# Block attention and a gated Fourier mixer in one kernel: two heads' outputs transposed into one half-word bank, block sums regrouped, zero products given banks of their own

## The chip, the core and the metric

The kernel runs on one NeuronCore of a Trainium2 chip. That core has a matrix engine (TensorE, PE in the profile), a vector engine (VectorE, DVE), a scalar engine (ScalarE, ACT), a general engine (GpSimd, POOL), and a queue engine (SyncE, SP) that only starts transfers. Each engine executes its own instructions strictly in the order in which the program lists them; engines wait for each other through semaphores. Products of TensorE land in PSUM, which is cut into banks; everything else lives in SBUF. The metric is the device time of one execution in microseconds (us); lower is better.

## The reference: what is computed

The input is `q`, `k`, `v` of shape (4, 8, 768, 64): 4 batches of 8 heads, 768 positions, 64 values each. Per head, the keys are cut into 12 blocks of 64 positions:

```python
k_rep = k.reshape(B, H, n_blocks, block, D).mean(axis=3)      # block sums of the keys
gate_scores = np.einsum('bhsd,bhnd->bhsn', q, k_rep)          # which blocks a query likes
top_idx = np.argsort(np.where(causal, gate_scores, -1e9), axis=-1)[..., -3:]
mask = own block or one of the top 3, and key position <= query position
attn = softmax(where(mask, q @ k.T / 8, -1e9)) @ v
x = attn.transpose(0, 2, 1, 3).reshape(4, 768, 512)
proj = x @ w_proj                                             # three parts: x1, x2, x3
y = x1 * irfft(rfft(x2) * rfft(filter)) * x3                  # along the 768 positions
out = y @ w_out
```

So there are 32 heads of attention, and after every 8 heads one batch of the mixer.

## The kernel before, in words

**Heads and slots.** The order of the work is written out by hand. The kernel runs through slots; slot 3n + s is step s (0, 1 or 2) of head n, written (n, s) here. In each slot the program lists, in this order: the scores of the slot's third of head n (`scores`, four, three or two products into a two-bank PSUM tile `sps`, then one exponential `ex` on ScalarE); at s = 1 the division of the head before by its row sums (`normalise`, VectorE, which writes `xn`); at s = 2 of every even n the transposition of two finished heads (`turn_outputs`); GpSimd's zeroing of the triangle above the diagonal in `ex` (`diagonals`, line 475); the work that prepares later heads (`prepare`); the mixer's pieces (`units`); and last the product of the previous slot's `ex` with the values (`product`, into the PSUM tile `o`, line 490).

**Mixer pieces.** A table (`head_plan`) gives each of the 24 slots of eight heads its pieces of the batch that is finished: X2 (the second projection), F1 and F2 (the Fourier products there and back), X13 (first and third projection) and O (the last product). The table starts at slot (9, 0), so that heads 9 to 16, 17 to 24 and 25 to 32 have the same pieces in the same places, except that the first of these rounds has no O.

**PSUM.** Two double banks (`ps_big`) hold the scores, and at the start the sine phases `dftp`. All other results share four single banks (`ps_one`, function `one_tile`): block sums, transposes, gates, masks, `o`, and the mixer's pairs of results. A new tile takes a bank whose last readers are listed earlier, and its first product waits for those readers. Two parts of one tile are not told apart when waits are placed.

**Outputs of two heads.** `turn_outputs` (lines 509 to 518) transposes `xn` (768 positions by 2 x 64 values) with TensorE in two halves of 384 positions, each into an fp32 bank of its own. The first half is multiplied by the identity, the second by a matrix `flip16` with ones on the other diagonal, which also turns the order of positions round, as the Fourier pieces want it. ScalarE copies each half into `xT`. GpSimd makes `flip16` in slot (1, 1).

**Block sums of the keys.** For heads 0 to 11 TensorE adds the keys up: `key_sums_mm`, then `key_sums_copy` (two copies on VectorE), `key_sums_turn` (transpose) and `key_sums_split`. For heads 12 to 31 they come from a second reading of the keys: `add_blocks` has GpSimd's transfer queue add four (or two) slices of the keys of a group of heads into `k_blk` (96 rows of 16 x 64 values), one transfer at the end of one of the heads listed in `by_block`; `fold_blocks` and `sum_blocks` halve the 16 slices down to one on VectorE (lines 325, 331, 335); `turn_blocks` transposes the result into `krt` (line 340, TensorE); `split_blocks` writes the two fp16 parts that `gate` multiplies with the queries. Groups: heads 12 to 15 (2 transfers), 16 to 23 (4), 24 to 31 (4). For a group that starts at head f the fold stands at (f - 3, 0), the sum at (f - 3, 1), the transpose at (f - 3, 2) and the split at (f - 2, 0): heads 9, 13 and 21.

**Gate and mask.** `gate` (at (n, 1), n even, for heads n + 2 and n + 3) picks the blocks on VectorE; `turn_mask` transposes the result into the bank `gmp`, and two copies (line 440) put it into the tile `qkT` of each of the two heads. Up to head 11 it stands at (n, 0), n odd, both copies on ScalarE; later at (n, 1), the second copy on VectorE.

**Zero products.** `warm` (line 755) multiplies zeros at the start, 5, 2 and 2 times. It writes the unused half of the second `dftp` tile. VectorE's `phase_round` (line 209) and `sines` (line 223) read and write the `dftp` tiles.

Of the kernel before, what the change touches and what calls it, by code (L numbers as in the profile page):

```python
# [12 lines left out]
ALU = mybir.AluOpType  # L13
# [4 lines left out]
def kernel(  # L18
# [30 lines left out]
    fp = FP16  # L49

    const = ctx.enter_context(tc.tile_pool(name="const", bufs=1))
# [21 lines left out]
    def one_tile(name, shape=(P, 512)):  # L73
        return ps_one.tile(list(shape), FP32, name=name, tag="one", padded_shape=[P, 512])
# [194 lines left out]
    def key_sums_mm(g, cs):  # L269

        w = len(key_groups[g])
        if g not in sums:
            sums[g] = one_tile("krp", (P, KG * D))
        for c in cs:
            nc.tensor.matmul(sums[g][0:NBLK, 0:w * D], lhsT=eblk[:, c, :], rhs=keys[g][:, 0:w, c, :],  # L275
                             start=(c == 0), stop=(c == SC - 1))

    def key_sums_copy(g):
        w = len(key_groups[g])
        krp = sums[g]  # L280
        krs = small.tile([NBLK, KG, 2, D], FP32, name="krs", tag="krs", bufs=1)
        nc.vector.tensor_copy(krs[:, 0:w, 0, :],
                              krp[0:NBLK, 0:w * D].rearrange("n (h d) -> n h d", h=w))
        nc.vector.tensor_copy(krs[:, 0:w, 1, :], krs[:, 0:w, 0, :])
        sums[g] = krs

    def key_sums_turn(g):
# [23 lines left out]
    HB = H * NBLK  # L311

    def add_blocks(j, i):
        first, w, parts, _ = by_block[j]
        b, h = divmod(first, H)
        src = k[b, h:h + w].rearrange("h (x t) d -> (h x) t d", t=64 // parts)
        if i == 0:
            blocks[j] = kpool.tile([HB, KP, D], FP32, name="k_blk", tag="k_blk", bufs=2)
        nc.gpsimd.dma_start(out=blocks[j], in_=src[:, i * KP:(i + 1) * KP, :],
                            accum_op=ALU.add if i else ALU.bypass)  # L320

    def fold_blocks(j):
        kb = blocks[j]
        m = KP // 2
        nc.vector.tensor_add(kb[:, 0:m, :], kb[:, 0:m, :], kb[:, m:KP, :])

    def sum_blocks(j):
        kb = blocks[j]
        m = KP // 4
        while m > 1:  # L330
            nc.vector.tensor_add(kb[:, 0:m, :], kb[:, 0:m, :], kb[:, m:2 * m, :])
            m //= 2
        krs = small.tile([HB, 2, D], FP32, name="krb", tag="krb", bufs=1)
        for i in range(2):
            nc.vector.tensor_add(krs[:, i, :], kb[:, 0, :], kb[:, 1, :])
        blocks[j] = krs
# [4 lines left out]
        blocks[j] = krt  # L341

    def split_blocks(j):
        first, w, parts, _ = by_block[j]
# [164 lines left out]
    def turn_outputs(m, xT):  # L509

        xn = xns.pop(m)
        for half in range(2):
            xp = one_tile("xp", (P, HALF))
            for i in range(HC):
                at_ = i if half == 0 else HC - 1 - i
                nc.tensor.matmul(xp[:, P * at_:P * (at_ + 1)], lhsT=xn[:, HC * half + i, :],
                                 rhs=flip16 if half else id_f16, start=True, stop=True)
            nc.scalar.copy(xT[:, m % DC, HALF * half:HALF * (half + 1)], xp)

# [229 lines left out]

    def warm(times):

        for _ in range(times):
            nc.tensor.matmul(phases["big", 1][:, 512:1024], lhsT=gm16s[1][:, 1, :],
                             rhs=gm16s[1][:, 2:SC, :].rearrange("p c s -> p (c s)"),
                             start=True, stop=True, skip_group_check=True)

    flip16 = const.tile([P, P], fp)
# [61 lines left out]

    def prepare(n, s):

        if s == 0:
            for m in key_loads.get(n, [n + 6]):
                if m < NH:
                    load_key(m)
            for m in [11, 12] if n == 6 else [n + 5] if n < 6 else [n + 6]:
                if m < NH:
                    load_query(m)  # L830
            if n + 2 < NH:
                load_value(n + 2)
        if n < 2:
            prepare_first(n, s)
        elif s == 0:
            if n % 2 == 1 and n + 1 < PE_HEADS:
                turn_mask([n + 1, n + 2], [nc.scalar.copy] * 2)
            if n + 2 in group_at:
                key_sums_turn(group_at[n + 2])
                key_sums_split(group_at[n + 2])  # L840
            if n == 2:
                turn_both(5)
            for j, group in enumerate(by_block):
                if n + 2 == group[0]:
                    split_blocks(j)
            if n + 4 < PE_HEADS:
                ready_query(n + 4)
            for j, group in enumerate(by_block):
                if n + 3 == group[0]:
                    fold_blocks(j)  # L850
        elif s == 1:
            if n in (6, 8, 10):
                spectrum(n // 2 - 3)
            if PE_HEADS <= n + 4 < NH:
                turn_query(n + 4)
            if PE_HEADS <= n + 5 < NH:
                cast_key(n + 5)
            if n % 2 == 0 and n < NH - 2:
                gate([n + 2, n + 3])
            elif PE_HEADS <= n + 1 < NH - 1:  # L860
                turn_mask([n + 1, n + 2], [nc.scalar.copy, nc.vector.tensor_copy])
            for j, group in enumerate(by_block):
                if n + 3 == group[0]:
                    sum_blocks(j)
        else:
            if n + 4 < PE_HEADS:
                turn_both(n + 4)
            if n + 1 < NH:
                cast_value(n + 1)
            for j, group in enumerate(by_block):  # L870
                for i, m in enumerate(group[3]):
                    if m == n:
                        add_blocks(j, i)

        if n > 0 and n + 3 in group_at:
            key_sums_mm(group_at[n + 3], (2 * s, 2 * s + 1))
            if s == 2:
                key_sums_copy(group_at[n + 3])

    def prepare_first(n, s):  # L880
        if (n, s) == (0, 0):
            turn_pe(1, 0, nc.vector.tensor_copy)
            gate([1])
            key_mask(2)
            ready_query(2)
            key_sums_mm(2, range(SC))
        elif (n, s) == (0, 1):
            turn_mask([1], [nc.scalar.copy])
            ready_query(3)
            key_sums_copy(2)  # L890
            key_sums_turn(2)
            turn_both(2)
            key_sums_split(2)
            for i in range(1, NB):
                nc.gpsimd.memset(v16s[i][:, :, D:DV], 1.0)
        elif (n, s) == (0, 2):
            turn_both(3)
            ready_query(4)
            cast_value(1)
        elif (n, s) == (1, 0):  # L900
            gate([2, 3])
        elif (n, s) == (1, 1):
            turn_both(4)
            ready_query(5)
            nc.gpsimd.memset(flip16, 0.0)
            nc.gpsimd.affine_select(
                out=flip16, in_=flip16, compare_op=ALU.not_equal,
                fill=1.0, base=-(P - 1), pattern=[[1, P]], channel_multiplier=1)
        else:
            turn_mask([2, 3], [nc.scalar.copy] * 2)  # L910
            cast_value(2)
# [3 lines left out]
    for slot in range(max(units) + 1):  # L915
# [32 lines left out]
        if s == 2:  # L948
            if PE_HEADS <= n + 5 < NH:
                cast_query(n + 5, nc.scalar.copy)  # L950
            for j, group in enumerate(by_block):
                if n + 3 == group[0]:
                    turn_blocks(j)

        pn, ps = divmod(slot - 1, 3)
# [36 lines left out]
```

## Time and profile before

| | |
|---|---|
| median of 3 runs | 269.45 us (268.19 to 270.83) |
| profiled execution: its own time | 268.72 us |
| profiled execution: span of the instructions | 267.0 us, mean granted TensorE clock 0.98 |
| busy: TensorE | 237.2 us (89% of the span) |
| busy: VectorE / ScalarE / GpSimd | 197.8 / 182.1 / 170.4 us |
| data moved | 41.05 MB, 154 GB/s on average |
| ScalarE's copies of the transposed outputs (line 518) | 32 of 485 ns |

The span runs from the first to the last instruction of the program; the execution's own time has 1.7 us around it. "Busy" adds up the time in which an engine had an instruction in work. In the lists of instructions, a row gives the start, the duration, engine and line, what is written and read, a count, and in brackets how long the engine stood idle before and who ended that wait. "PEld" is TensorE's loading of weights, which runs beside its products.

### The profile page before, as it was taken

The page shows a single profiled execution, that of the slowest core. Times are in us where ns is not written, and L with a number is a line of the kernel's source. Part 1 is how long each engine was busy: PE and PEld are TensorE (multiplying, and loading weights), DVE is VectorE, ACT ScalarE, POOL GpSimd, SP SyncE. Part 2 cuts the span into 40 slices and gives each one's busy share as a digit, 9 for nine tenths or more (in the row PEclk, how much of TensorE's full clock was granted, in tenths as well). Part 3 has the DMA queues.
Part 4 walks back from the last instruction along what each step waited for, and adds up shares of the span by engine and source line. Part 5 has one row for each costly group of instructions (what it writes and reads, how often), then busy time and mean ns, then how long its engine had stood idle before and what let it go on. Part 6 is the DMA issues. An engine that isn't in the chain of part 4 may idle for free.

```text
span 267.0 us, 6284 instructions
## 1 busy us (share of the span) xinstructions
PE 237.2 (89%) x2214; PEld 144.5 (54%) x2214; DVE 197.8 (74%) x592; ACT 182.1 (68%) x283; POOL 170.4 (64%) x326
## 2 busy tenths in 40 slices
PE   7778888989788888699999988999999999999994
PEld 3447655646445555466565554565555655554641
DVE  4875798887779889976787999677878635588730
ACT  3545786879878676768887766887866785522463
POOL 5635666677735788779866986877567657228330
PEclk9897999999999999979999999999999999999999
DMA  8977876999799999988999995898382120110056
GB/s 166 217 118 206 209 169 114 185 164 200 122 227 163 180 187 199 221 181 179 195 191 239 201 203 128 204 222 193 73 195 74 26 79 2 39 39 2 0 198 237
DMA packets 115232, 41.05 MB, mean 154 GB/s; under 512 B 107328, under 2 KB 110400, under 8 KB 115200
## 3 DMA queue, kind: packets, MB, share of 16 engines
q1 hardware_dynamic: 110880, 34.61, 62.0%
q0 software_dynamic: 4320, 6.03, 14.2%
q8 instruction: 17, 0.28, 0.5%
q14 instruction: 15, 0.12, 0.2%
HBM read 28.57 MB, written 6.29 MB: 131 GB/s over the span
## 4 chain that ended last, share of the span: by engine, by line
PE 45%; DVE 22%; ACT 15%; POOL 7%; issue 7%; DMA 3%; SPq 0%; ACTq 0%; POOLq 0%; DVEq 0%
ACT ex L467 7%; PE sps L464 6%; PE op L620 6%; PE o L490 4%; PE x13b L585 4%; POOL ex L475 3%; DMA q_nat<-in_q_dram 3%; PE x2a L546 3%; PE x2b L546 3%; ACT qkT L440 3%; DVE t L570 3%; DVE t L567 2%; PE f2b L601 2%; PE krp L275 2%; DVE m L423 2%
## 5 line engine op out<-in xcount | busy, mean ns | idle before, releaser
L467 ACT ACTIVATE ex<-sps 128x1024 f16<-128x1024 f32 (+2 forms) x96 | 87.3, 918 | 44.1 <-PE sps L464 38.7
L475 POOL TENSOR_SCALAR_AFFINE_SELECT ex<-ex 128x128 f16<-128x128 f16 (+1 forms) x128 | 47.8, 387 | 58.1 <-ACT ex L467 57.2
L464 PE MATMUL sps<-qkT 76*128 76x384 f16 (+2 forms) x288 | 53.0, 292 | 0.5 <-ACT qkT L440 0.5
L490 PEld LDWEIGHTS <-ex 128*128 128x128 f16 x672 | 32.4, 99 | 20.6 <-issue 6.0
L490 PE MATMUL o<-v,ex 128*128 128x65 f16 x672 | 36.9, 195 | 3.6 <-POOL ex L475 0.9
L585 PEld LDWEIGHTS <-wp 128*128 128x128 f16 x256 | 24.5, 97 | 18.1 <-issue 4.4
L585 PE MATMUL x13b<-xT,wp 128*128 128x384 f16 x108 | 21.9, 325 | 2.2 <-DVE t L570 1.7
L464 PEld LDWEIGHTS <-qkT 76*128 76x128 f16 x288 | 20.6, 98 | 5.2 <-issue 0.8
L620 PE MATMUL op<-wo,yT 128*128 128x512 f16 x96 | 23.0, 378 | 0.0
L613 POOL TENSOR_TENSOR yT<-gx,yy 128x384 f16<-128x384 f32 x16 | 17.5, 1091 | 8.1 <-DVE yy L607 8.1
L585 PE MATMUL x13a<-xT,wp 128*128 128x384 f16 x108 | 22.0, 325 | 0.0
L574 POOL TENSOR_TENSOR PQ<-t,t 128x512 f16<-128x512 f32 x12 | 15.3, 1271 | 8.1 <-DVE t L567 7.5
L379 POOL TENSOR_SCALAR qk<-rem 128x320 f16<-128x320 f32 x32 | 15.4, 481 | 6.9 <-DVE rem L375 4.7
L590 DVE TENSOR_TENSOR gx<-x1sb,x13b 128x384 f32<-128x384 f16 x27 | 14.9, 551 | 5.8 <-ACT x1sb L589 4.8
L506 DVE TENSOR_TENSOR xn<-o,rz 128x384 f16<-128x384 f32 x32 | 17.8, 558 | 1.1
L375 DVE TENSOR_TENSOR rem<-q_nat,qk 128x320 f32<-128x320 f32 x32 | 17.3, 541 | 1.3 <-ACT qk L368 0.3
L623 ACT COPY osb<-op 128x512 f32<-128x512 f32 x24 | 14.0, 585 | 5.7 <-PE op L620 5.0
L357 POOL CAST qk<-k_nat 128x384 f16<-128x384 f32 x31 | 16.5, 534 | 0.0
L401 POOL CAST v<-v_nat 128x384 f16<-128x384 f32 x32 | 16.2, 506 | 0.1
L440 ACT COPY qkT<-gmp 12x640 f16<-12x640 f16 x22 | 15.0, 681 | 1.4 <-PE gmp L438 0.9
L575 POOL TENSOR_TENSOR PQ<-t,t 128x512 f16<-128x512 f32 x12 | 15.2, 1268 | 0.0
L546 PEld LDWEIGHTS <-xT 128*128 128x128 f16 x96 | 9.2, 97 | 9.6
(152 smaller groups left out, 483.4 us busy)
## 6 DMA issues: line engine op xcount, KB each, us to landing
q_nat<-in_q_dram SPq DMA_DIRECT2D x32, 192.0 KB, 3.9
k_nat<-in_k_dram SPq DMA_DIRECT2D x32, 192.0 KB, 4.0
v_nat<-in_v_dram SPq DMA_DIRECT2D x32, 192.0 KB, 4.0
out_dram<-osb SPq DMA_DIRECT2D x24, 256.0 KB, 2.1
k_blk<-in_k_dram POOLq DMA_DIRECT2D x10, 384.0 KB, 6.0
rows<-in_moe_filter_fft_dram SPq DMA_DIRECT2D x2, 768.0 KB, 6.6
wp<-in_moe_w_proj_dram POOLq DMA_DIRECT2D x6, 256.0 KB, 5.4
wo<-in_moe_w_out_dram POOLq DMA_DIRECT2D x2, 256.0 KB, 8.0
```

Source lines behind the costliest of these rows:

```text
L357: copy(qk16s[n % NB][:, 1, :, 0:D], keys[g][:, i])
L375: nc.vector.tensor_sub(rems[n], q_nat[:, 1:SC], qk16[:, 0, 1:SC, 0:D])
L440: copies[h](turned[n][D:D + NBLK, 0, 1:SC], gmp[64 * h:64 * h + NBLK, P:S].rearrange("n (c s) -> n c s", c=SC - 1))
L464: nc.tensor.matmul(sps[:, col:col + qe - qs], lhsT=turned[n][0:76, 1, kc, :], rhs=qT[0:76, qs:qe], start=True, stop=True, skip_group_check ...
L467: nc.scalar.activation(ex[:, lo:hi], sps[:, lo:hi], AF.Exp, bias=0.0, scale=scale)
L475: nc.gpsimd.affine_select(out=sub, in_=sub, compare_op=ALU.is_ge, fill=0.0, base=0, pattern=[[0, cnt], [1, P]], channel_multiplier=-1)
L490: nc.tensor.matmul(outs[n][:, qc * DE:(qc + 1) * DE], lhsT=ex[:, col + P * j:col + P * (j + 1)], rhs=vals[n][:, kc, 0:DE], start=(gi == 0 ...
L506: nc.vector.tensor_tensor(out=xns[n // 2][:, :, D * (n % 2):D * (n % 2 + 1)], in0=o[:, :, 0:D], in1=rz.to_broadcast([P, SC, D]), op=ALU.mult)
L546: nc.tensor.matmul(pp, lhsT=xT[:, dc, base + P * i:base + P * (i + 1)], rhs=wp[:, dc, Dm:2 * Dm], start=(dc == 0), stop=(dc == DC - 1))
L585: nc.tensor.matmul(dst, lhsT=wp[:, dc2, base:base + P], rhs=xT[:, dc2, hs:hs + HALF], start=(dc2 == 0), stop=(dc2 == DC - 1))
L613: nc.gpsimd.tensor_mul(yT[:, dc, S - 1:HALF - 1:-1], st["g"][:, dc, 1, :], yy[:, 1, :])
L620: nc.tensor.matmul(op, lhsT=yT[:, cc, P * scn:P * (scn + 1)], rhs=wo[:, cc, :], start=(cc == 0), stop=(cc == DC - 1))
```

## The change

Six edits:

1. `turn_outputs` transposes all six pieces by the identity into one fp16 tile of 768 columns, which is one bank. ScalarE copies the first 384 columns forwards and the last 384 backwards. `flip16` and the two GpSimd instructions that make it go.
2. The groups of block sums become heads 12 to 19, 20 to 27 (4 transfers each) and 28 to 31 (2). Each group names its four places: fold, sum, transpose, split. They are (9, 0), (9, 1), (9, 2), (10, 0); then (15, 0), (15, 1), (15, 2), (17, 0); then (23, 0), (23, 1), (23, 2), (25, 0). Transfers are issued at the end of heads 4, 5, 6, 7; 10, 11, 12, 13; 17, 19.
3. In a slot, fold, sum and split now stand ahead of the rest of `prepare`, so the sum is listed before the mask copies.
4. The mask of heads 10 and 11 moves from (9, 0) to (9, 1), its second copy from ScalarE to VectorE.
5. The two copies of the block sums of heads 2 and 3 move from VectorE in (0, 1) to ScalarE in (0, 0).
6. `warm` takes a single bank (`unread`) for each of its three calls.

```diff
-    by_block = [(12, 4, 2, [6, 7]), (16, 8, 1, [8, 9, 10, 11]), (24, 8, 1, [13, 15, 17, 19])]
+    by_block = [
+        (12, 8, 1, [4, 5, 6, 7], [(9, 0), (9, 1), (9, 2), (10, 0)]),
+        (20, 8, 1, [10, 11, 12, 13], [(15, 0), (15, 1), (15, 2), (17, 0)]),
+        (28, 4, 2, [17, 19], [(23, 0), (23, 1), (23, 2), (25, 0)]),
+    ]
...
-    def key_sums_copy(g):
+    def key_sums_copy(g, copy=nc.vector.tensor_copy):
...
-        for half in range(2):
-            xp = one_tile("xp", (P, HALF))
-            for i in range(HC):
-                at_ = i if half == 0 else HC - 1 - i
-                nc.tensor.matmul(xp[:, P * at_:P * (at_ + 1)], lhsT=xn[:, HC * half + i, :],
-                                 rhs=flip16 if half else id_f16, start=True, stop=True)
-            nc.scalar.copy(xT[:, m % DC, HALF * half:HALF * (half + 1)], xp)
+        xp = ps_one.tile([P, S], fp, name="xp", tag="one", padded_shape=[P, 2 * 512])
+        for c in range(SC):
+            nc.tensor.transpose(xp[:, P * c:P * (c + 1)], xn[:, c, :], id_f16)
+        nc.scalar.copy(xT[:, m % DC, 0:HALF], xp[:, 0:HALF])
+        nc.scalar.copy(xT[:, m % DC, HALF:S], xp[:, S - 1:HALF - 1:-1])
...
+        unread = one_tile("unread")
         for _ in range(times):
-            nc.tensor.matmul(phases["big", 1][:, 512:1024], lhsT=gm16s[1][:, 1, :],
+            nc.tensor.matmul(unread, lhsT=gm16s[1][:, 1, :],
...
     def prepare(n, s):
 
+        for j, group in enumerate(by_block):
+            for fn, place in zip((fold_blocks, sum_blocks, None, split_blocks), group[4]):
+                if (n, s) == place and fn:
+                    fn(j)
...
-            if n % 2 == 1 and n + 1 < PE_HEADS:
+            if n % 2 == 1 and n + 1 < 10:
                 turn_mask([n + 1, n + 2], [nc.scalar.copy] * 2)
...
-            elif PE_HEADS <= n + 1 < NH - 1:
+            elif 10 <= n + 1 < NH - 1:
                 turn_mask([n + 1, n + 2], [nc.scalar.copy, nc.vector.tensor_copy])
...
             key_sums_mm(2, range(SC))
+            key_sums_copy(2, nc.scalar.copy)
         elif (n, s) == (0, 1):
             turn_mask([1], [nc.scalar.copy])
             ready_query(3)
-            key_sums_copy(2)
...
-            nc.gpsimd.memset(flip16, 0.0)
-            nc.gpsimd.affine_select(
-                out=flip16, in_=flip16, compare_op=ALU.not_equal,
-                fill=1.0, base=-(P - 1), pattern=[[1, P]], channel_multiplier=1)
...
             for j, group in enumerate(by_block):
-                if n + 3 == group[0]:
+                if (n, s) == group[4][2]:
                     turn_blocks(j)
```

More of the change, by code (lines that the diff above doesn't have):

```diff
@@ L281, in key_sums_copy @@
         krs = small.tile([NBLK, KG, 2, D], FP32, name="krs", tag="krs", bufs=1)
-        nc.vector.tensor_copy(krs[:, 0:w, 0, :],
-                              krp[0:NBLK, 0:w * D].rearrange("n (h d) -> n h d", h=w))
-        nc.vector.tensor_copy(krs[:, 0:w, 1, :], krs[:, 0:w, 0, :])
+        copy(krs[:, 0:w, 0, :], krp[0:NBLK, 0:w * D].rearrange("n (h d) -> n h d", h=w))
+        copy(krs[:, 0:w, 1, :], krs[:, 0:w, 0, :])
         sums[g] = krs
@@ L313, in add_blocks @@
     def add_blocks(j, i):
-        first, w, parts, _ = by_block[j]
-        b, h = divmod(first, H)
-        src = k[b, h:h + w].rearrange("h (x t) d -> (h x) t d", t=64 // parts)
+        first, w, parts = by_block[j][0:3]
+        t = 64 // parts
+        src = k.rearrange("b h (x t) d -> (b h x) t d", t=t)[first * S // t:(first + w) * S // t]
         if i == 0:
@@ L343, in split_blocks @@
     def split_blocks(j):
-        first, w, parts, _ = by_block[j]
+        first, w, parts = by_block[j][0:3]
         krt = blocks.pop(j)
@@ L859, in prepare @@
                 gate([n + 2, n + 3])
-            elif PE_HEADS <= n + 1 < NH - 1:
+            elif 10 <= n + 1 < NH - 1:
                 turn_mask([n + 1, n + 2], [nc.scalar.copy, nc.vector.tensor_copy])
-            for j, group in enumerate(by_block):
-                if n + 3 == group[0]:
-                    sum_blocks(j)
         else:
@@ L870, in prepare @@
             for j, group in enumerate(by_block):
-                for i, m in enumerate(group[3]):
-                    if m == n:
-                        add_blocks(j, i)
+                if n in group[3]:
+                    add_blocks(j, group[3].index(n))
         if n > 0 and n + 3 in group_at:
@@ L951 @@
             for j, group in enumerate(by_block):
-                if n + 3 == group[0]:
+                if (n, s) == group[4][2]:
                     turn_blocks(j)
```

6 lines of the change are left out of this document (removed).

## The prediction, made before the changed kernel was run

> **What bounds the kernel now.** I read the page first, for the engines' shares:
>
> ```profile
> PE 237.2 (89%) x2214; PEld 144.5 (54%) x2214; DVE 197.8 (74%) x592; ACT 182.1 (68%) x283; POOL 170.4 (64%) x326
> ```
>
> TensorE has work in 89% of the span, and no other engine is near that. So what can go is TensorE's idle time, about 30 us, and the second view is that of its waits (total us, times, longest):
>
> ```profile
> PE krt L291 <- DVE krs L284: 3.0, 3, 1.9
> PE krt L340 <- DVE krb L335: 2.1, 2, 1.0
> ...
> PE f2b L601 <- ACT xT L518: 1.5, 3, 0.5
> PE f1b L562 <- ACT xT L518: 1.4, 4, 0.3
> ...
> PE gps L414 <- DVE krb L307: 0.9, 1, 0.9
> ```
>
> Each of these waits has an edit beside it in the diff. TensorE executes in order, so a wait in it delays all that is listed behind, the next scores first. Third came the list of instructions around each wait, fourth the granted clock in single stretches.
>
> **The change part by part**, against the profiled execution's own 268.72 us.
>
> *Zero products (edit 6).* In the list of the start:
>
> ```profile
> 3.01 2.31 PE L755 MATMUL dftp<-gm 128*128 128x512 f16 x5
> ...
> 5.36 1.02 DVE L209 TENSOR_SCALAR dft_ka<-dftp 128x384 f32<-128x384 f32 x2 [1.69 <-PE dftp L755]
> ...
> 6.64 0.86 PE L395 MATMUL tp<-id_f,qk 128*76 128x128 f16 x6
> ...
> 8.37 0.23 PE L291 MATMUL krt<-id_f,krs 12*128 12x12 f32 x1 [0.86 <-DVE krs L284]
> ```
>
> VectorE stood 1.69 us for products that nobody reads, because they share a tile with a phase. In the changed program the second and third rounding carry no wait for TensorE. VectorE's queue behind them (query, remainder, block sums) moves forward by up to 1.6 us. Next late is TensorE itself: its zero products and the transposes still end at 7.50. So `krt` comes at 7.50 instead of 8.37: **-0.85 us**. Bounds: nothing (if a later wait of the start decides) and -1.6 (the whole rounding). The three new bank users add no wait: their banks come from block sums and transposes whose readers the next TensorE instruction needs anyway.
>
> *Copies on ScalarE (edit 5).* Head 0:
>
> ```profile
> 18.43 0.92 ACT L467 ACTIVATE ex<-sps 128x896 f16<-128x896 f32 x1 [2.15 <-PE sps L464]
> ...
> 19.38 0.68 ACT L440 COPY qkT<-gmp 12x640 f16<-12x640 f16 x1
> ...
> 20.69 0.26 PE L291 MATMUL krt<-id_f,krs 12*128 12x12 f32 x2 [1.92 <-DVE krs L284]
> ...
> 22.05 0.65 PE L490 MATMUL o<-v,ex 128*128 128x65 f16 x8
> ```
>
> The sums' products are listed ahead of the scores for which the exponential at 18.43 waited, so they are done by then; but VectorE copies them only after a gate and two queries. ScalarE idles just there (2.15 us before 18.43), and the copies go there. They have 128 columns; ScalarE's copies of 384 take 485 ns (row below), so I take 0.3 us each, which push the exponential from 18.43 to about 18.6. Behind them wait the mask copy (to 20.3) and with it, by its bank, the product `o`, which thus starts at 20.3 instead of 22.05: **-1.7 us**. Bounds: -1.9 (the whole wait) and -0.5 (if VectorE's transposed copies, now first in its queue, come late for head 1).
>
> *Mask of heads 10 and 11 (edit 4).*
>
> ```profile
> 74.21 0.47 PE L438 MATMUL gmp<-id_f,gm 128*76 128x128 f16 x5 [1.02 <-DVE gm L427]
> ```
>
> At (9, 1) the gate is long done, and X2 starts without it: **-1.0 us**, bounds -0.5 and -1.4. VectorE gets one 0.49 us copy more in head 9, beside TensorE's X2.
>
> *Block sums leave heads 13 and 21 (edits 2, 3).* Starts of heads by their first exponential, with what stands between:
>
> ```profile
> 103.28 1.02 ACT L467 ACTIVATE ex<-sps 128x1024 f16<-128x1024 f32 x1 [0.90 <-POOL ex L475]
> ...
> 107.72 1.26 POOL L575 TENSOR_TENSOR PQ<-t,t 128x512 f16<-128x512 f32 x1
> ...
> 108.17 1.41 DVE L331 TENSOR_TENSOR k_blk<-k_blk 96x256 f32<-96x256 f32 x2
> ...
> 110.41 0.27 PE L340 MATMUL krt<-id_f,krb 96*128 96x96 f32 x1 [1.04 <-DVE krb L335]
> ...
> 111.44 1.83 ACT L467 ACTIVATE ex<-sps 128x1024 f16<-128x1024 f32 x2 [1.62 <-PE sps L464]
> ...
> 207.82 1.02 ACT L467 ACTIVATE ex<-sps 128x1024 f16<-128x1024 f32 x1 [1.22 <-PE sps L464]
> ...
> 214.00 1.02 ACT L467 ACTIVATE ex<-sps 128x1024 f16<-128x1024 f32 x1 [0.72 <-PE sps L464]
> ```
>
> Head 13 lasts 8.16 us (103.28 to 111.44). Head 29 has the same mixer pieces and no sums, and lasts 6.18. In heads 13 and 21 the sums stand on VectorE behind the mask copy, which waits for ScalarE, and `krt` holds TensorE for 1.04 us in both (the 2.1 in the waits). The split then holds the gate of head 14 for 0.9. All three go, since group 20 to 27 is split at (17, 0) and used at (18, 1): **-3.0 us**. Bounds: -3.9 (1.98 in each head) and -1.5.
>
> *They arrive in heads 15 and 23.* There:
>
> ```profile
> 119.14 0.55 DVE L590 TENSOR_TENSOR gx<-x1sb,x13b 128x384 f32<-128x384 f16 x1 [0.65 <-ACT x1sb L589]
> ...
> 119.83 0.56 DVE L506 TENSOR_TENSOR xn<-o,rz 128x384 f16<-128x384 f32 x1
> ...
> 120.20 1.00 POOL L612 TENSOR_TENSOR yT<-gx,yy 128x384 f16<-128x384 f32 x1
> ...
> 121.15 0.99 POOL L613 TENSOR_TENSOR yT<-gx,yy 128x384 f16<-128x384 f32 x1
> ...
> 121.26 0.49 DVE L440 COPY qkT<-gmp 12x640 f16<-12x640 f16 x1 [0.86 <-ACT qkT L440]
> ...
> 121.78 0.56 DVE L590 TENSOR_TENSOR gx<-x1sb,x13b 128x384 f32<-128x384 f16 x1
> ...
> 122.26 0.65 PE L601 MATMUL f2b<-inv,PQ 128*128 128x384 f16 x3
> ```
>
> The fold fits into the idle 0.65 us. In head 13 the sums took from 108.17 until shortly before `krt` at 110.41, 2.1 us; started behind `xn` at 120.4 they end at 122.5. The 0.86 us of idle time takes part of it; the mask copy then ends near 123.0 instead of 121.75 and the next multiplication near 123.6. In the changed program the second half of F2 waits for that copy and `krt` for that multiplication. TensorE, which began that half at 122.26, would have reached `krt` some 0.5 us later. Taken with the little that the next head makes up, **+1.2 us each, +2.4**. Bounds: nothing (the sums as short as in head 9) and 1.98 each, what they cost in head 13. The held bank is counted below; the splits at (17, 0) and (25, 0) lie beside X2, where VectorE waits for TensorE.
>
> Head 9's sums show that the price is not fixed:
>
> ```profile
> 78.65 0.79 DVE L331 TENSOR_TENSOR k_blk<-k_blk 96x256 f32<-96x256 f32 x2
> ```
>
> The same two adds took 0.79 us there and 1.41 in head 13, where GpSimd's L575 ran over their start until 108.98. [...]
>
> *The clock.*
>
> ```profile
> 17.60:21.04 3.44, 1.52 (x16) 0.85 (x15) 2.74 (x8) 1.60 (x2) 2.04 (x5) 1.00 0.29 67
> 21.04:24.46 3.42, 3.42 (x35) 3.12 (x34) 1.39 (x4) 1.61 (x2) 0.41 (x3) 0.50 0.87 226
> 106.40:109.80 3.40, 2.93 (x23) 1.36 (x21) 2.87 (x7) 3.25 (x6) 3.32 (x5) 1.00 1.37 200
> 109.80:113.20 3.40, 1.88 (x31) 1.44 (x31) 3.30 (x10) 1.78 (x3) 2.06 (x6) 1.00 1.14 244
> 113.20:116.60 3.40, 3.26 (x22) 2.12 (x22) 2.80 (x15) 1.96 (x5) 3.23 (x6) 0.50 0.80 177
> ```
>
> (First the length, then TensorE's busy time; after POOL's the granted clock.) The two stretches with 1.52 and 1.88 us of work are each followed by one at half clock; 2.93 us of work is not. Edits 2 and 5 fill both. A half-clock stretch of 3.4 us loses at most 1.7; I count half, 0.8 each: **-1.6 us**. Bounds: -3.4, and +1.7 if a new pause in head 15 brings one. [...]
>
> *One bank for the outputs (edit 1).* F1's and F2's second halves wait 2.9 us in seven even heads for ScalarE's copy of the first half, whose bank they take. With one bank less in use they find another, except in heads 16 and 24, where `krt` holds one until the split. There they now wait for both copies. The copies:
>
> ```profile
> L518 ACT CAST xT<-xp 128x384 f16<-128x384 f32 x32 | 13.9, 485 | 0.2
> ...
> L397 ACT COPY qkT<-tp 128x768 f16<-128x768 f16 x10 | 8.0, 800 | 3.5 <-PE tp L395 3.5
> ```
>
> -2.9, +0.5 (head 24 keeps its wait), +0.49 in each of heads 16 and 24: **-1.4 us**. The time passes on, since ScalarE waits for TensorE at the next head's first exponential (1.22 us at 207.82, 0.72 at 214.00). Half words cost 400 ns (half of 800) to 485. No row shows ScalarE reading backwards; nearest are GpSimd's forward and backward writes, L612 and L613 above, at 1.00 and 0.99. So I take 485, bounds 400 and 970 (twice). Twice would show only where TensorE needs the second half: heads 16, 24 and the end, +1.5. The six transposes cost what six products cost. At the end the first copy waits for all six: **+0.2**.
>
> *The rest.* `flip16` is off GpSimd's queue, whose wait for exponentials hides it (next row): nothing, or -0.5 without that cover. Two more transfers, in heads 4 and 5, cost GpSimd some 0.8 us each:
>
> ```profile
> POOL ex L475 <- ACT ex L467: 57.2, 48, 4.2
> ```
>
> ```profile
> L319 POOL DMA_DIRECT2D k_blk<-in_k_dram x10: 553/803/917, 61.4 to 149.0; - x10
> ...
> DMA to landing us min/median/max: 5.0/6.0/7.3
> ```
>
> Each adding transfer waits on GpSimd's queue for the one before; behind it stands the zeroing of the next head. Heads last 6 us and more, as long as a landing, and GpSimd waits on average 1.2 us (57.2 in 48) before a zeroing. I take nothing; bounds nothing and 1.5 at each of seven places.
>
> Sum: -0.85 - 1.7 - 1.0 - 3.0 + 2.4 - 1.6 - 1.4 + 0.2 = -6.95, so **261.8 us**. The median shown, 269.45, lies 0.7 above the profiled execution; I leave the forecast on the latter.
>
> **The rivals.** (a) *The sums cost as much in heads 15 and 23.* GpSimd's multiplication holds VectorE's adds until 122.14 and more; TensorE waits 1.98 instead of 1.2 in each (+1.6), and the clock falls behind each as it did (+1.6): 265.0. For it: L331's rows. Against: VectorE has 0.65 and 0.86 us idle in head 15. (b) *The start gives back.* VectorE or ScalarE, not TensorE, sets heads 0 and 1, and edits 5 and 6 yield 0.5 instead of 2.55: with (a), 267.1. For it: VectorE's 2.74 us of work in 17.60 to 21.04. Against: it loses two copies there. (c) *Slower: GpSimd stuck behind adding transfers.* Place: from head 4 to 7 and 10 to 13, where the weights load too. It decides from a landing of about 7.5 us (a head plus GpSimd's idle time); at 9 us it is 1.5 us at each of seven places, +10.5: 272.3. Against: the longest landing is 7.3. (d) *The backward read is several times slower.* At four times, 1.5 us more in each of 16 copies against 0.7 to 1.2 of ScalarE's idle time before the next exponential, some +0.8 each: 274.6. Against: the pair 1.00 and 0.99. (e) *The clock does not follow short pauses*: the half-clock stretches stay, only shifted: 263.4. Against: both lie right behind a stretch of little work.
>
> **How the numbers follow.** Forecast, 258 to 263: 0.48. (a) 0.18, (b) 0.12, (c) 0.07, (d) 0.05, (e) 0.10. Range 257.5 to 268: it leaves (c) and (d) outside and some of the terms' ends taken together. One per cent of 269.45 is 2.7 us, about what a measurement of this kernel can tell from no change. Faster by more, below 266.8: the forecast, (a), (e) and a part of (b), 0.81; within: the rest of (b), 0.09; slower: most of (c) and (d), 0.10.
>
> **What would show it.** VectorE's second rounding has no wait for TensorE. `krt` of head 0 follows the mask at once. Heads 13 and 21 last about 6.2 us, heads 15 and 23 about 7.1. L601's and L562's waits for `xT` remain in heads 16 and 24 alone. No stretch at half clock near head 14. The second copy of `xT` lasts 400 to 490 ns. Wrong I would be with a wait of equal size behind each that goes, or a GpSimd that idles for landings.

## The result, and the profile after

The changed kernel takes 261.31 us (median, 260.9 to 261.67) against 268.98 us before (268.19 to 270.83). The ratio is 0.9705, 95% interval 0.9651 to 0.9759. The forecast was 261.8 us, inside a range of 257.5 to 268. The total came out right; the sections below show that several of its terms were wrong, in opposite directions.

The profiled execution took 260.9 us, with a span of 259.2 us (267.0 before). The page of the changed kernel, engines' shares and the row of the granted clock:

```profile
span 259.2 us, 6281 instructions
PE 230.9 (89%) x2214; PEld 141.5 (55%) x2214; DVE 198.7 (77%) x591; ACT 181.7 (70%) x284; POOL 169.6 (65%) x324
PEclk9999999999999999999999999999999999999999
```

TensorE has the same 2214 matmuls and 6.3 us less busy time (237.2 before). The products did not become fewer, but three stretches of 3.41 us in which they ran at half clock are gone; the third row has 90% or more of the full clock in every slice. Half of these 10.2 us, 5.1 us, is the most that the clock can explain of the 6.3; the rest was not traced. The other 1.5 us by which the span is shorter are idle time. The view of waits of the changed kernel (total us, times, longest) shows what left and what came:

```profile
POOL k_blk L322 <- DMA k_blk<-in_k_dram: 3.2, 3, 2.3
...
PE o L493 <- POOL ex L478: 3.0, 6, 1.3
...
PE f2b L602 <- DVE qkT L443: 2.1, 2, 1.1
...
PE f2b L602 <- ACT xT L519: 1.5, 2, 0.9
...
PE gps L417 <- DMA qkT<-qk: 1.1, 1, 1.1
```

The waits of `krt` for VectorE, 3.0 and 2.1 us, are no longer in the view, nor is that of `f1b` for `xT`. Of the rows shown, four are new or larger. The second half of F2 waits for the mask copy. The product `o` waits 3.0 us for GpSimd's zeroing (0.9 before). The gate of head 14 waits for a transfer. And GpSimd stands 3.2 us for landings.

The lengths of the heads, each worked out as the difference of two neighbouring first exponentials (us), place these rows. Beside the two kernels stand two experiments that are used further down:

| heads | before | after | after without edits 2, 3 | sums one slot later |
|---|---|---|---|---|
| start and 0 | 25.34 | 20.73 | 20.82 | 20.66 |
| 7 and 8 | 10.76 | 11.63 | 10.62 | 11.46 |
| 9 | 8.76 | 7.25 | 7.60 | 7.34 |
| 13 and 14 | 14.43 | 12.30 | 13.79 | 12.30 |
| 15 and 16 | 11.47 | 13.27 | 11.47 | 12.33 |
| 21 and 22 | 13.99 | 12.34 | 13.79 | 12.61 |
| 23 and 24 | 12.13 | 14.17 | 11.72 | 12.44 |

From before to after: -4.6 at the start, +0.9 in heads 7 and 8, -1.5 in head 9, -2.1 and -1.65 where the sums left, +1.8 and +2.0 where they arrived. The other heads, most of them even ones of the mixer, give 2.6 us. What follows the last head's start is 47.5 us in both.

### The profile page after: what moved, and what is told of

Its sections match the earlier page's. It is cut to its first block, busy times and chain, and to the rows that moved or that the text cites. A ratio compares the mean times of both kernels' runs of the same rounds, so it can differ in the third digit from the quotient of the medians.

```text
span 259.2 us, 6281 instructions
## 1 busy us (share of the span) xinstructions
PE 230.9 (89%) x2214; PEld 141.5 (55%) x2214; DVE 198.7 (77%) x591; ACT 181.7 (70%) x284; POOL 169.6 (65%) x324
## 4 chain that ended last, share of the span: by engine, by line
PE 48%; DVE 18%; ACT 14%; POOL 7%; issue 6%; DMA 5%; ACTq 0%; DVEq 0%; POOLq 0%
PE sps L467 8%; PE op L621 6%; ACT ex L470 6%; DMA k_blk<-in_k_dram 5%; PE o L493 4%; PE x13b L586 4%; PE x2b L547 4%; PE x2a L547 3%; ACT qkT L443 3%; DVE t L568 3%; DVE t L571 2%; POOL ex L478 2%; DVE t L567 2%; PE f2b L602 2%; PE krp L279 2%
## 5 line engine op out<-in xcount | busy, mean ns | idle before, releaser
L478 POOL TENSOR_SCALAR_AFFINE_SELECT ex<-ex 128x128 f16<-128x128 f16 (+1 forms) x128 | 48.2, 397 | 48.3 <-ACT ex L470 47.5
L467 PE MATMUL sps<-qkT 76*128 76x384 f16 (+2 forms) x288 | 52.3, 289 | 0.7 <-ACT qkT L443 0.5
L382 POOL TENSOR_SCALAR qk<-rem 128x320 f16<-128x320 f32 x32 | 14.6, 457 | 7.3 <-DVE rem L378 5.1
L443 ACT COPY qkT<-gmp 12x640 f16<-12x640 f16 x21 | 14.3, 680 | 0.9 <-PE gmp L441 0.4
```

The costliest lines, as they stand in the source:

```text
L443: copies[h](turned[n][D:D + NBLK, 0, 1:SC], gmp[64 * h:64 * h + NBLK, P:S].rearrange("n (c s) -> n c s", c=SC - 1))
L467: nc.tensor.matmul(sps[:, col:col + qe - qs], lhsT=turned[n][0:76, 1, kc, :], rhs=qT[0:76, qs:qe], start=True, stop=True, skip_group_check ...
L478: nc.gpsimd.affine_select(out=sub, in_=sub, compare_op=ALU.is_ge, fill=0.0, base=0, pattern=[[0, cnt], [1, P]], channel_multiplier=-1)
```

## The experiments

Ratios are against the kernel before, run beside each.

**Edit 6 alone** (`warm` writes to a bank of its own).

```
-            nc.tensor.matmul(phases["big", 1][:, 512:1024], lhsT=gm16s[1][:, 1, :],
+        unread = one_tile("unread")
...
+            nc.tensor.matmul(unread, lhsT=gm16s[1][:, 1, :],
```

> The kernel before with edit 6 alone (zero products in banks of their own). Theory (the terms of the prediction, and the clock follows short stretches of little TensorE work): the mask transposes of head 0 come 0.85 us earlier or more, and the half-clock stretch near 11 us goes while those near 22 us and near 113 us stay, so -0.9 to -2.5 us. Rival (b), VectorE or ScalarE sets heads 0 and 1: the first exponential comes earlier, but head 1 starts as before, within 0.5 us of before. Rival (e), the clock does not follow short stretches: half-clock stretches as before, only shifted, -0.9.

Measured: 267.09 us against 268.6, ratio 0.993 (0.9891 to 0.9969). TensorE's list in this kernel:

```profile
7.43 0.28 PE L291 MATMUL krt<-id_f,krs 12*128 12x12 f32 x1
...
19.16 0.26 PE L291 MATMUL krt<-id_f,krs 12*128 12x12 f32 x2 [0.38 <-DVE krs L284]
```

The first turn comes at 7.43 in place of 8.37: 0.94, where 0.85 was counted. But the third turn (head 0) comes 1.53 us earlier too, and its wait fell from 1.92 to 0.38, without edit 5. VectorE's queue, moved forward by the roundings, brings the copies sooner. Edits 5 and 6 thus pay in part for the same wait, and with edit 6 in place 0.38 of it is left for edit 5. Head 1 starts 2.62 us earlier, so rival (b) falls. The half clock did not go as expected: there is none near 21 us, the stretch at the start lies at 14.48 in place of 10.80, that near 113 us stays, and two that the kernel before has not come at 58.85 and 72.50.

**Edit 5 alone** (sums of heads 2 and 3 copied by ScalarE).

```
             key_sums_mm(2, range(SC))
+            key_sums_copy(2, nc.scalar.copy)
...
-            key_sums_copy(2)
```

> The kernel before with edit 5 alone (sums of heads 2 and 3 copied by ScalarE). Theory: the wait of 1.92 us in head 0 goes, the head is 1.7 us shorter, and the half-clock stretch that follows it at 21 us goes too: -1.7 to -2.6 us. Rival (b): VectorE sets head 0; a new wait of TensorE for its transposed copies takes the place, -0.5. Rival (e): the wait goes and a half-clock stretch stays near 21 us: -1.7.

Measured: 266.88 us, ratio 0.9914 (0.9883 to 0.9946). The wait is gone and head 0 lasts 8.59 in place of 10.08. How much of that is the wait can't be read from this profile: TensorE was at half clock from 12.88 to 19.71, so the turn came at 20.53 although it did not wait, and nothing was at half clock behind it. The time, 1.7 us below before by the medians, is the theory's and not rival (b)'s 0.5.

**Edit 1 alone** (outputs in one bank, second half copied backwards; the hunk on `turn_outputs` of the change, and `flip16` removed).

> The kernel before with edit 1 alone (outputs of two heads in one bank, second half copied backwards). Theory: the waits of the second halves of F1 and F2 for ScalarE's copy (2.9 us in seven even heads) go and the time passes on: -1.2 to -2.4 us. Rival, the wait goes but the next head takes the time back: within 0.5 us. Rival (d) in a small form, the backward copy is slower than the other by over 0.3 us: slower by 0.2 to 1 us.

Measured: 265.26 us, ratio 0.9877 (0.9832 to 0.9922): -3.3 us, more than any expectation, at 1.2 in the forecast. All of `f1b`'s and `f2b`'s waits for `xT` are gone from its view of waits, and so is that of the transposes `tp` behind `xp` in head 2. Heads 18, 26 and 28 are 0.5 us shorter each, head 30 0.67, head 24 0.41.

**Edits 2 and 3 alone** (block sums regrouped and placed by a list).

```
-    by_block = [(12, 4, 2, [6, 7]), (16, 8, 1, [8, 9, 10, 11]), (24, 8, 1, [13, 15, 17, 19])]
+        (12, 8, 1, [4, 5, 6, 7], [(9, 0), (9, 1), (9, 2), (10, 0)]),
+        (20, 8, 1, [10, 11, 12, 13], [(15, 0), (15, 1), (15, 2), (17, 0)]),
+        (28, 4, 2, [17, 19], [(23, 0), (23, 1), (23, 2), (25, 0)]),
```

> The kernel before with edits 2 and 3 alone (block sums regrouped and moved). By the terms of the prediction: heads 13, 14, 21 and 22 give 3.0 and heads 15 and 23 take 2.4, and the half-clock stretch near 113 us goes: -0.6 to -1.4 us. By what the profile of the changed kernel shows, heads 13, 14, 21, 22 give 3.8 and heads 15, 16, 23, 24 take 3.8 back, since the sums cost as much beside GpSimd's multiplications as before (rival a): 0, within 0.8 us, and in heads 15 and 23 TensorE waits 1 us or more for the mask copy that stands behind the sums.

Measured: 271.15 us, ratio 1.0053 (1.0009 to 1.0097): half a per cent slower, with an interval that just leaves out 1, where the forecast's terms made it faster. In its view of waits `f2b` waits 2.4 us in two places for the mask copy. Heads 13, 14, 21 and 22 give 3.9 us and heads 15, 16, 23 and 24 take 4.3. Heads 7 and 8 last 10.81 us, as before, although GpSimd stands 2.7 us for landings.

**Edit 4 alone** (mask of heads 10 and 11 at (9, 1): `n + 1 < 10` and `10 <= n + 1` in place of `PE_HEADS`).

> The kernel before with edit 4 alone (mask of heads 10 and 11 turned at (9, 1)). Theory: the wait of 1.02 us ahead of X2 in head 9 goes, head 9 is 1.0 to 1.5 us shorter (7.25 us, as heads 17 and 25) and nothing is given back: -1.0 to -1.5 us. Rival: the second copy, now on VectorE, makes VectorE late in head 10, whose products wait longer: within 0.5 us.

Measured: 267.86 us against 268.68, ratio 0.995 (0.9906 to 0.9994). Head 9 is 1.43 us shorter and head 10 0.38 longer: -1.05, the forecast's 1.0.

**The change without edits 2 and 3**, and **without edit 1** (the hunks above taken back in the changed kernel).

> The changed kernel without edits 2 and 3 (block sums grouped and placed as in the kernel before). By the forecast's terms the two are worth 0.6 us and 0.8 us of clock: 262.0 to 262.7. By what the head lengths of the two profiles show (heads 13, 14, 21 and 22 gave 3.8, of it 0.65 by the clock; heads 15, 16, 23 and 24 took 3.8, heads 7 and 8 0.9) they cost about 1.5 us without the clock: 259.8 to 261. Heads 13 and 21 at 8.1 us, 15 and 23 at 5.95, 7 and 8 together 0.5 us or more shorter than in the changed kernel.

> The changed kernel without edit 1 (outputs of two heads in two banks, the second half turned by the products). By the forecast's term, edit 1 is worth 1.2 us: 262.5. By the head lengths of the even heads and by edit 1 alone (-3.3), it is worth 2.4 to 3.3: 263.7 to 264.6, with the waits of the second halves of F1 and F2 for ScalarE's copy back in heads 18, 20, 22, 26, 28 and 30.

Measured against 268.63: 260.04 us without 2 and 3, ratio 0.9671 (0.9603 to 0.974); 265.3 us without edit 1, ratio 0.9874 (0.9817 to 0.9931). The first can't be told from the changed kernel's 0.9705 by the times; the head table shows what it consists of. Against that column the changed kernel gains 1.49 and 1.45 in heads 13, 14, 21 and 22 and loses 1.80 and 2.45 in heads 15, 16, 23 and 24 and 1.01 in heads 7 and 8. So edits 2 and 3 brought nothing here; by these heads they cost 2.3 us. The second run makes edit 1 worth 4.0 us, of which some is clock: its profile has two half-clock stretches. The waits of `f1b` and `f2b` for `xT` are back in it, 1.4 and 1.5 us.

**What a backward read costs.**

```
-        nc.scalar.copy(xT[:, m % DC, HALF:S], xp[:, S - 1:HALF - 1:-1])
+        nc.scalar.copy(xT[:, m % DC, HALF:S], xp[:, HALF:S])
```

> The changed kernel, with the second copy of xT reading its half of the bank forwards; the second half of each sequence then stands in the wrong order, so the turning is left out. It prices the backward read alone. Theory: the copy falls from 496 ns by at most 25 ns, and the time stays within 0.5 us of the changed kernel. Rival (d) in a small form: a forward copy is 400 ns or less, and the even heads become shorter, -1 us or more.

The groups of the changed kernel, then of this one (busy us, mean ns):

```profile
L519 ACT COPY xT<-xp 128x384 f16<-128x384 f16 x16 | 7.9, 496 | 0.0
...
L518 ACT COPY xT<-xp 128x384 f16<-128x384 f16 x16 | 7.6, 474 | 0.3 <-PE xp L517 0.3
```

```profile
L519 ACT COPY xT<-xp 128x384 f16<-128x384 f16 x16 | 7.9, 495 | 0.0
```

The second copy takes 495 ns forwards and 496 backwards. The 22 ns over the first copy are not the direction. Rival (d) is out. The time, 262.72 us (ratio 0.974, 0.9666 to 0.9813), can't be told from the changed kernel's. Its median is 1.4 us higher, more than the 0.5 expected; its profile has two half-clock stretches, at 9.72 and 67.75, which the changed kernel's has not.

**The sums in the X2 heads 17 and 25** (first added line), **and one slot later** (second); the group of head 28 alike, in heads 23 to 26.

```
-        (20, 8, 1, [10, 11, 12, 13], [(15, 0), (15, 1), (15, 2), (17, 0)]),
+        (20, 8, 1, [10, 11, 12, 13], [(17, 0), (17, 1), (17, 2), (18, 0)]),
+        (20, 8, 1, [10, 11, 12, 13], [(15, 0), (15, 2), (16, 2), (17, 0)]),
```

> The changed kernel, with the block sums of the second and third group moved from heads 15 and 23 to heads 17 and 25 (the X2 heads, as the first group has them in head 9), the splits one head later. Theory: in X2 heads VectorE waits for TensorE and GpSimd has no two-input instruction beside the adds, so the two adds take 0.8 us in place of 1.4 and hide; the waits for the mask copy (1.05 and 1.09 us) and, since krt no longer holds a bank over heads 16 and 24, the waits for the second copy of xT (0.57 and 0.89 us) go: heads 15, 16, 23 and 24 give 3.4 to 3.9 us back, so -3 to -4 us against the changed kernel, about 257.7, that is -11 us against before. Rival: the sums cost TensorE their 2 us in X2 heads as well: heads 17 and 25 become 1 to 2 us longer, 260 to 262.

> The changed kernel, with the sums of the second and third group moved one slot later (behind the mask copy in heads 15 and 23) and krt one head later, at (16, 2) and (24, 2). It tells the two costs of these heads apart: what the mask copy waits for, and the bank that krt holds. Theory: no wait for the mask copy in heads 15 and 23, these heads are back at 6.0 us (-1.4 each); in heads 16 and 24 krt takes a bank just ahead of the second half of F2 or behind it, and the next split comes at once; -2.0 to -3.5 us against the changed kernel. The adds themselves run after GpSimd's multiplications and take 0.8 us in place of 1.4. Rival: VectorE is simply full in heads 15 and 16 (the sums are 2.6 us of it), so TensorE waits as long one slot later: within 0.7 us of the changed kernel.

Measured: in X2 heads 261.57 us, ratio 0.9692 (0.9625 to 0.9758), no gain; one slot later 258.73 us, ratio 0.9615 (0.9548 to 0.9682). VectorE and GpSimd in head 15 of the changed kernel:

```profile
112.75 1.42 DVE L334 TENSOR_TENSOR k_blk<-k_blk 96x256 f32<-96x256 f32 x2
114.21 1.14 DVE L338 TENSOR_TENSOR krb<-k_blk 96x64 f32<-96x64 f32 x2
115.38 0.49 DVE L443 COPY qkT<-gmp 12x640 f16<-12x640 f16 x1
```

```profile
112.79 1.23 POOL L613 TENSOR_TENSOR yT<-gx,yy 128x384 f16<-128x384 f32 x1
113.99 1.04 POOL L614 TENSOR_TENSOR yT<-gx,yy 128x384 f16<-128x384 f32 x1
114.98 0.29 POOL L478 TENSOR_SCALAR_AFFINE_SELECT ex<-ex 128x128 f16<-128x128 f16 x1
```

and TensorE there:

```profile
115.92 0.65 PE L602 MATMUL f2b<-inv,PQ 128*128 128x384 f16 x3 [1.05 <-DVE qkT L443]
```

The four adds take 2.6 us from 112.75 on, while GpSimd multiplies beside them until 115.03; the mask copy and `f2b` stand behind. One slot later:

```profile
113.62 0.49 DVE L443 COPY qkT<-gmp 12x640 f16<-12x640 f16 x1 [0.87 <-ACT qkT L443]
114.14 0.56 DVE L591 TENSOR_TENSOR gx<-x1sb,x13b 128x384 f32<-128x384 f16 x1
114.61 0.74 DVE L334 TENSOR_TENSOR k_blk<-k_blk 96x256 f32<-96x256 f32 x2
115.38 0.65 DVE L338 TENSOR_TENSOR krb<-k_blk 96x64 f32<-96x64 f32 x2
```

```profile
113.75 1.00 POOL L614 TENSOR_TENSOR yT<-gx,yy 128x384 f16<-128x384 f32 x1
114.70 0.48 POOL L478 TENSOR_SCALAR_AFFINE_SELECT ex<-ex 128x128 f16<-128x128 f16 x1
```

The same four adds take 1.4 us; the multiplication ends at 114.75, 0.14 us behind their start, and GpSimd's zeroing beside them takes 0.48 us (0.29 in the changed kernel at 114.98); the mask copy runs 1.8 us earlier, `f2b` waits no more, and head 15 is back at 5.95. Of this the place in the queue and the shorter adds were not tried apart. Head 16 is 0.51 longer than in the changed kernel: its gate waits 0.87 for the queries' transfer. In the X2 heads the rival came true: heads 15, 16, 23 and 24 give back 4.3 us, but heads 17 and 25 last 0.95 and 1.17 longer and heads 18 and 26 0.46 and 0.80. The 0.9 that is left was lost again at the start, to a half-clock stretch of 1.8 us in the profile. Why these heads grew shows in that kernel's VectorE, GpSimd and TensorE:

```profile
127.08 1.55 DVE L334 TENSOR_TENSOR k_blk<-k_blk 96x256 f32<-96x256 f32 x2
```

```profile
127.03 1.00 POOL L614 TENSOR_TENSOR yT<-gx,yy 128x384 f16<-128x384 f32 x1
```

```profile
129.78 1.02 PE L547 MATMUL x2b<-wp,xT 128*128 128x512 f16 x4 [0.70 <-DVE qkT L443]
```

I had expected no GpSimd multiplication there. Head 17 still has one, that of F2's last unit, until 128.0; two of the adds take 1.55 us beside it (1.42 in head 15 of the changed kernel), and X2 waits 0.70 for the mask copy behind them; the gate in head 18 waits 0.30 for the later split. Head 9, where the first group's adds take 0.8 us, has no F2 ahead of it.

**The adding transfers spaced** (on top of the version above: heads 2, 4, 5, 7 in place of 4, 5, 6, 7).

> The kernel with the sums one slot later (e7_behind), with the four transfers of the first group in heads 2, 4, 5 and 7 in place of 4, 5, 6 and 7. Theory (a small form of rival (c)): GpSimd stands for landings, 3.2 us in three places, and with it the zeroing that TensorE's products wait for (1.54, 0.54 and 0.51 us in heads 6 to 8); two of the three waits go, heads 6 to 8 are 0.5 to 1.0 us shorter in sum. Rival: another wait takes their place in these heads (the filter spectrum, which TensorE waits for in before too): no difference beyond 0.3 us.

Measured: 258.43 us, ratio 0.96 (0.9544 to 0.9655); by the times not to be told from the version before it. GpSimd in the changed kernel, at the transfer listed at the end of head 7, and TensorE behind it:

```profile
64.96 0.85 POOL L322 DMA_DIRECT2D k_blk<-in_k_dram  x1 [2.28 <-DMA k_blk<-in_k_dram]
65.56 1.03 POOL L478 TENSOR_SCALAR_AFFINE_SELECT ex<-ex 128x256 f16<-128x256 f16 x2
```

```profile
66.64 0.42 PE L493 MATMUL o<-v,ex 128*128 128x65 f16 x8 [1.27 <-POOL ex L478]
```

and the row of waits in the spaced kernel:

```profile
POOL k_blk L322 <- DMA k_blk<-in_k_dram: 1.6, 1, 1.6
```

Spaced, GpSimd waits once and not three times, and heads 7 and 8 last 10.62 us in place of 11.46. This version is the fastest of those measured: 1.1% below the changed kernel by the two ratios, whose intervals just touch.

**Filling the pauses without removing them** (the kernel before; `fill` issues products of `id_f16` that nobody reads, into the bank of the turn and ahead of it, in head 0 and head 13).

```
+        if g == 2:
+            fill(bank, 20)
...
+        if j == 1:
+            fill(bank, 10)
```

> The kernel before with products that nobody reads put ahead of two of the turns of block sums: 20 products of 128 columns in head 0 (where TensorE waits 1.92 us) and 10 in head 13 (where it waits 1.04 us), in the bank that the turn takes anyway. The waits themselves stay. Theory (a 3.4 us stretch in which TensorE works less than about 2 us is followed by one at half clock): the half-clock stretches at 21 us and at 113 us go, that at 11 us stays, and the time falls by 0.8 to 1.7 us with fewer runs above 270. Rival (e): the half-clock stretches stay, and the time is as before or up to 0.5 us longer.

Measured: 268.94 us, ratio 1.001 (0.9977 to 1.0043): no gain, so the expectation failed in its sum. Its stretches (length, then TensorE's busy time; the granted clock behind POOL's):

```profile
17.80:21.22 3.42, 2.85 (x40) 2.26 (x40) 2.46 (x7) 1.60 (x2) 2.05 (x6) 1.00 0.38 87
21.22:24.63 3.41, 3.12 (x54) 2.55 (x52) 2.66 (x8) 3.02 (x4) 1.34 (x3) 1.00 0.91 244
41.94:45.35 3.41, 2.24 (x35) 1.24 (x32) 3.17 (x12) 2.37 (x4) 2.37 (x6) 1.00 1.07 207
45.35:48.76 3.41, 3.37 (x19) 2.18 (x20) 2.11 (x14) 1.61 (x4) 1.51 (x3) 0.50 1.24 206
110.21:113.62 3.41, 2.21 (x41) 1.72 (x41) 3.31 (x10) 1.83 (x2) 2.04 (x6) 1.00 0.95 212
113.62:117.03 3.41, 3.41 (x24) 2.06 (x21) 2.56 (x14) 2.43 (x5) 3.33 (x7) 0.50 1.10 182
```

In head 0 the theory held: 2.85 us of work, no half clock behind it, and the head is 1.55 us shorter although the turn still came at 20.50. In head 13 the fill reached only 2.21 us, and the half clock stayed. Another stretch came at 45.35 behind 2.24 us of work, and head 4 is 1.43 longer. One profile can't say how often the stretch at 45 comes. But the mean granted clock of the ten executions is 0.981, against 0.986 over the eighteen of the kernel before: by this the fill left no less half clock than there was. Why it came in other places stays open.

## Why the prediction was right, point by point

The sum was -6.95 us. The medians give -7.67, the two profiled executions -7.82.

*Zero products, -0.85, and copies on ScalarE, -1.7.* The signs came as named. In the changed kernel (VectorE; TensorE):

```profile
3.12 1.49 DVE L213 TENSOR_SCALAR dft_ka<-dftp 128x384 f32<-128x384 f32 x3 [0.66 <-PE dftp L208]
```

```profile
16.80 0.45 PE L441 MATMUL gmp<-id_f,gm 128*12 128x128 f16 x5
17.18 0.29 PE L294 MATMUL krt<-id_f,krs 12*128 12x12 f32 x2
```

The three roundings run without a stop, and the turn of head 0 follows the mask at once, 3.5 us earlier than before (20.69). Head 1 starts 4.6 us earlier, where these two terms and 0.8 of clock came to 3.35. What is over is clock, by an estimate: the two stretches of the start, priced from other runs below at 0.47 and 1.55, leave 2.6 for the two terms, which were 2.55. Their sum was right and their split was not. The step that failed is the whole 1.7 put down to edit 5: edit 6 by itself brought the wait of that turn from 1.92 to 0.38.

*The clock, -1.6.* Right in kind, short in size. Three half-clock stretches are gone, not two: that at 10.8 to 14.22 also went, which the prediction left in place. And the step "I count half, 0.8 each" was too small where TensorE is the bound. The fill in head 0 gained 1.55 for one stretch. The kernel with the sums in X2 heads, which has the changed kernel's instructions up to head 8, fell into one stretch from 14.96 to 18.37 and started head 1 at 22.54 in place of 20.73: 1.8 us. One from 9.72 to 13.14, in the kernel with the forward copy, cost 0.47 there (21.20). The spaced kernel took 256.87 us in its execution at a clock of 1.00 and 258.15 to 259.06 in the three at 0.993, which is one stretch. In head 14, where TensorE also waits for others, a stretch cost 0.64 (6.28 before, 5.64 without edits 2 and 3). For the three that went, 0.47, 1.55 and 0.64 make an estimate of 2.7 us. Rival (e) fell: in head 0, where a step with little work was filled to 2.85 us, no half clock followed.

*Mask, -1.0.* Right: -1.05 alone.

*Sums leave heads 13 and 21, -3.0.* Right: 1.49 and 1.45, against the kernel without edits 2 and 3. Not quite as described: heads 13 and 21 last 6.8 us, not 6.2, for `x13b` waits 0.67 at their start for the products of F1, which it did before; and the gate of head 14 found a new wait at once:

```profile
106.28 0.29 PE L417 MATMUL gps<-krb,qkT 128*128 128x24 f16 x5 [1.07 <-DMA qkT<-qk]
```

A transfer that transposes the queries had been hidden behind the split.

*They arrive in heads 15 and 23, +2.4.* Too small: 1.45 and 1.49 in these heads. The step that failed is "started behind `xn` at 120.4 they end at 122.5": the adds took the 2.6 us of the changed kernel's rows above, not 2.1. This was rival (a) in kind, adds that last longer beside a multiplication; its price of 1.98 in each head and its half clock did not come. With the held bank, which the prediction counted in another term (+0.5 and twice +0.49), heads 15, 16, 23 and 24 lost 4.25 us, against the kernel without edits 2 and 3, in place of 3.9. The two adds into `k_blk` took 1.42 and 1.55 us beside a multiplication and 0.74 where it had all but ended, and there the zeroing beside them took 0.48 in place of 0.29. What ties the two engines together here is not shown.

*One bank for the outputs, -1.4 (with the end, -1.2).* Too small: 3.3 alone. The step that failed is "+0.5 (head 24 keeps its wait), +0.49 in each of heads 16 and 24", for the bank that `krt` holds. That charge belongs to edits 2 and 3: without edit 1 these heads are as long (5.98 and 6.84, against 5.87 and 6.73). Its size was about right: heads 16 and 24 are 0.35 and 0.55 longer than before, where 0.49 each was counted. The 2.9 of the seven even heads were 3.2, in the kernel without edits 2 and 3. The copy itself was priced well (485 for 496 measured, though the signs named had 490 at most), the end's +0.2 did not show.

*The rest, 0.* Wrong by 1.0: rival (c) came true in small. The transfers land up to 7.0 us after their issue and follow each other 6.6 to 7.6 us apart; GpSimd's queue stood for 2.28 us before the zeroing quoted above, and `o` behind it for 1.27 (the longest in the row of waits, 1.3). The price is not fixed: with edits 2 and 3 alone heads 7 and 8 paid nothing for 2.7 us of such waits. In the kernel with the forward copy one such wait lasted 3.00, TensorE stood 1.99 ahead of `o`, half clock followed, and the two heads lasted 12.82.

So the sum held because the sums' arrival and the adding transfers, some 1.4 us too cheap, were met by the clock (1.1 by the estimate), the outputs (0.5) and heads 9 and 10, which together gave 1.7 where 1.0 was counted. That they met this closely is luck.

## What to carry to other kernels

Moving work to an engine's idle gap is priced by what stands behind it in that queue and by what the neighbour engine does at that moment: the same four adds took 2.6 us in one slot and 1.4 us in the next. Undo each part in the changed kernel, not only add it to the old one: the part that moved the most work was the one that cost. And where TensorE's idle time is cut, count the clock as well as the wait: here it gave 2.7 of the 7.67 us, by the estimate above.

## What the runs showed of the hardware

In these profiles half-clock stretches begin on a grid of 3.41 us. Within one execution all starts fall on one grid (10.80, 21.04 and 113.20 before: 3 and 30 steps); between executions its offset differs (first starts at 14.48 with edit 6 alone, 12.88 with edit 5 alone, 9.72 with the forward copy). In the eleven profiles that have one such stretch before 240 us, which fixes the grid, I worked out TensorE's busy time in all steps at full clock between 6 and 240 us, 708 in all. With at most 2.06 us of work, 18 of 19 are followed by half clock; from 2.07 to 2.25, 5 of 18; above, 1 of 671. (Steps shifted by 0.01 us move single ones from one class to the next.) One of the least worked, in the kernel with the forward copy, and then the two least worked steps of the changed kernel, whose grid is fixed by a half-clock stretch at 258.75, behind its last products:

```profile
64.33:67.75 3.42, 1.43 (x23) 0.94 (x21) 2.23 (x6) 2.11 (x4) 1.63 (x3) 1.00 0.34 44
67.75:71.16 3.41, 3.41 (x29) 2.51 (x30) 1.80 (x14) 2.06 (x5) 1.95 (x5) 0.50 1.00 142
```

```profile
6.16:9.57 3.41, 2.26 (x29) 1.45 (x27) 2.19 (x8) 1.70 (x3) 2.67 (x10) 1.00 1.37 218
64.19:67.60 3.41, 2.14 (x39) 1.66 (x38) 2.42 (x6) 2.19 (x4) 2.48 (x6) 1.00 0.41 41
```

Neither of these two is followed by half clock. The longest pause in a step ahead of one of these half-clock stretches is 1.99 us, in the kernel with the forward copy. Steps with two fifths of their time (1.35 us) or more without work were followed by half clock 18 times of 19, those with about a third (1.16 to 1.34 us) 5 times of 18, whether it was one wait (1.92 us, up to 20.69 before) or several short ones (none over 0.51 in the filled kernel's step at 41.94). Whether this accounts for the scatter of the kernel before (267.55 to 271.33 over its runs, against 0.8 us over the four of the changed one) is not shown: of its executions those at a mean clock of 0.994 took 268.5 to 268.7 us, and some at 0.987 only 267.6.
